# Gate steps moved to GpSimd, the first q and k loaded from two queues, and a per-step rank table in a fused attention and expert kernel

## The chip, the core and the metric

The kernel runs on one core of one Trainium2 chip. The metric is the time of one execution on the device in microseconds. Three timed runs of the kernel before gave 886.53, 890.16 and 890.55 us; their median, 890.16 us, is what the changed kernel is compared with. The engines are named as in the profile: PE is TensorE, DVE VectorE, ACT ScalarE, POOL GpSimd, SP SyncE (here a DMA queue).

## The reference

Attention over 8 batches of 8 heads, 576 positions and head size 64, in which scores further than `tau` below their row's maximum are dropped, and behind it a mixture of 8 experts on the 4608 rows of 512 that come out:

```python
scores = scale * np.matmul(q, k.transpose(0, 1, 3, 2))
thresh = np.max(scores, axis=-1, keepdims=True) - tau
scores = np.where(scores >= thresh, scores, -1000000000.0)
attn = np.exp(scores - np.max(scores, axis=-1, keepdims=True))
x = np.matmul(attn / (np.sum(attn, axis=-1, keepdims=True) + 1e-09), v)   # per head
...
do_compute = x @ w_skip > 0            # out = x elsewhere
logits = xc @ w_gate                   # xc = x[do_compute], 8 logits a token
e_idx = np.argmax(logits, axis=1)
for e in range(E):
    h = np.maximum(xc[mask] @ w1[e], 0.0)
    y[mask] = gate_w[mask, None] * (h @ w2[e])
out[do_compute] = xc + y
```

## The kernel before

**Attention.** Two heads make a pair (`g`, 32 in all, four to a batch). A pair has four chunks of 128 rows with two units each (one per head) and a ninth unit, the tail of 64 rows of both heads. A unit is a score block of 128 x 576 in one of three PSUM buffers `sps`: PE makes it (`score`, L601), DVE takes the maximum (`top`, L612), ACT the exponential (`expo`, L624), DVE multiplies it with the threshold mask (`mask`, L632), which frees the buffer. ACT rounds the chunk's `p` to f16 (`fph`, tile `hla`, L412), POOL makes the remainder (`fpl`, the split step, L683), SP transposes both by DMA (`turn`, L688, tile `PTa`), and PE multiplies with V (`av`, L751). The tail goes through PE instead (`tr` L705, `hi`, `lo` L713). V is brought to two f16 parts for each batch by `plan_v`: an absolute sum in two halves (`fsum`, ACT L494 or DVE L496), a scale (`fr`, ACT L555 or POOL L558), a cast, a remainder. `plan_out` copies the product out (`cpy`), makes the reciprocal (`fr`, L794) and on POOL the output rows `xb` (`fx`, L803) and tails `x` (`ft`, L816). `plan_logits` transposes these on PE (L859) and adds up the router's logits (L885).

**Gate.** For every two batches `plan_gate` turns nine logit columns a partition into expert, weight and slot of each token: a chain of small steps on tiles `ca` (128 x 72) and `gw` (128 x 9), all on DVE (L984 to L1080) but for the exponential (ACT) and a count over partitions (`rank`, PE), and at its end nine indirect DMAs from POOL (`sca`, L1108). The last two batches get two gates, one for batch 6, one for the rest. Behind batch 6's gate `plan_pick` chooses the fullest expert; `plan_early` loads its w1 in two halves (`lw`, and `second`, which is the load `raw` in L397), splits the weights in two parts (`hi` on ACT, `lo` on POOL, L1260), gathers 320 of its tokens (`ga`, L401) and runs its first layer (`L1`, PE L1311).

**Experts.** Behind the planned part, expert after expert in a fixed order; TensorE is busy nearly all of that time.

**What sets the order.** All of it up to the end of the first layer is recorded as steps with engines, durations and dependences. `Plan.run` (a list scheduler in Python, at build time) then goes through the steps: for each engine it looks at those that would be ready within `LOOK` = 0.1 us of the earliest, takes the one with the smallest key, and emits its instructions. So the keys order steps that compete for an engine, and each engine, SP's and POOL's queue too, works its instructions off in that order. A step that lists several engines goes to the one that can start it first. A key is a sum of named offsets from `ORDER`, with up to four values, chosen by the pair's place in its batch:

```python
pair = int(max(key.at, 0)) // STEP
return sum(c * ORDER[n][pair % len(ORDER[n])] for n, c in key.offs) if key.offs else key.at
```

`lock=True` marks DVE steps that the planner doesn't start while POOL is busy with a step of its own.

**Start.** SP issues the first pair's two loads (`load` in `plan_pair`, L437 and L438) as the first step of the plan. `warm` (L1407) keeps PE busy with 14 products of `ident` until the data is there.

Of the kernel before, what the change touches and what calls it, by code (L numbers as in the profile page):

```python
# [18 lines left out]
ALU = mybir.AluOpType  # L19
# [51 lines left out]
DLAT = 1.9  # L71
ORDER = dict(
    gk=(4349, 1.58e+04, 0, 0,),
    vm=(5384, 0, 0, 0,),
    tt2=(613.7, 1.58e+04, -3.449e+04, -1512,),
    hi2=(-4.346e+04, 3.034e+05, 3.133e+05, -5282,),
    lo2=(562.8, -2.259e+04, -9.309e+04, -4.515e+04,),
    eg=(-7406, -2.093e+05, 0, 0,),
    L1m=(2.989e+05,),
    ex=(-8.448e+04, 1.427e+04, -3.875e+04, -2e+04,),  # L80
    eav=(-1.313e+05, -1.651e+04, 4.278e+04, 1.964e+04,),
    ld=(-3.456e+04, 1.596e+05, -1.641e+05, 6.358e+04,),
    qs=(1.122e+05, 1717, -9.452e+04, 1.214e+04,),
    S=(-2.225e+05, -1.566e+05, -2.312e+04, -9.311e+04,),
    mx=(5534, 2.237e+05, -6.53e+04, -6820,),
    th=(-3.468e+04, 1.915e+05, -1.495e+05, 6.269e+04,),
    e=(-1.451e+05, -6.782e+04, -2141, -1.003e+04,),
    p=(-9031, -1.426e+04, -1.807e+05, -1.63e+05,),
    ph=(-1322, 1.222e+05, 4.057e+05, -9.705e+04,),
    pl=(-1.781e+05, 4.205e+04, 6250, -6.626e+04,),  # L90
    tt=(-2.69e+05, 6405, -2703, 9.818e+04,),
    av=(3.22e+05, 2.029e+04, 3.147e+04, 3.456e+04,),
    cp=(1.287e+04, -3.512e+04, -6.049e+04, -1.725e+05,),
    x=(-2.958e+04, -4.386e+04, 0.001192, 4.233e+04,),
    xw=(2433, 1831, 1.558e+04, -1.251e+05,),
    row=(-1594, 0, 0, 0,),
    rsp=(-1.029e+05, 0, 0, 0,),
    init=(-2.381e+05,),
    L1=(-1.868e+05,),
    sc=(-1.345e+05,),  # L100
    d0=(-1.107e+04,),
    v=(0.000848, 0, 0, -9374,),
    vsp=(-0.0004024, 0, 0, -1.917e+05,),
    V2=(0.002816, 0, 0, 0,),
    GS=(3.047e-10,),
)


class Key:


    def __init__(self, at=0.0, offs=()):
        self.at, self.offs = at, tuple(offs)

    def __add__(self, x):
        x = x if isinstance(x, Key) else Key(x)
        return Key(self.at + x.at, self.offs + x.offs)

    def __mul__(self, a):
        return Key(self.at * a, [(n, c * a) for n, c in self.offs])  # L120

    def __sub__(self, x):
        return self + x * -1

# [1774 lines left out]
```

## Time and profile before

| | |
|---|---|
| timed runs | 886.53, 890.16, 890.55 us (median 890.16) |
| the profiled execution | 882.97 us, its span 881.2 us |
| attention stage | from the first scores at 7.7 us to the last product with V at about 605 us |
| first layer of the early expert starts | 619.88 us |
| experts | to the end of the span |

The profile is of one execution. Its span is the time from the first to the last instruction; 1.8 us of the execution lie around it. "Busy" is the time in which an engine worked on an instruction; matmuls overlap, so PE's figure is an upper bound. A wait is idle time of an engine ahead of an instruction, with the instruction that ended it.

### The profile page before, as it was taken

To read this page: it belongs to the slowest core of one execution; us is meant where nothing else is said; L and a number is where in the kernel's file an instruction comes from. 1 tells how busy PE (TensorE), PEld (TensorE's weight loads), DVE (VectorE), ACT (ScalarE), POOL (GpSimd) and SP (SyncE) were. 2 spreads that over 40 slices of the span, in tenths; PEclk is the share of its full clock that TensorE was granted. 3 is DMA by queue.
4 is the path that set the end of the run, shared out by engine and by line. 5 is a ranking of instruction groups with operands and counts; after the bars stand their busy time and mean duration, and the time that the engine had idled before them with its cause. 6 is when DMAs were issued, how large, how long until landed. Compare 5 with 4: busy or idle time off the path is not lost. (4 is left out here: it accounts for less than half of the span.)

```text
span 881.2 us, 19509 instructions
## 1 busy us (share of the span) xinstructions
PE 790.0 (90%) x7294; PEld 668.1 (76%) x7294; DVE 680.2 (77%) x1284; ACT 602.9 (68%) x941; POOL 579.3 (66%) x384
## 2 busy tenths in 40 slices
PE   7789989888989997998988898774999999999997
PEld 5577868776867776786876777663879898999986
DVE  7988988898989799888989989881445463487772
ACT  5888978987988896897898788564334352454451
POOL 4767857857977784897685799468253464374453
PEclk9999999999999999999999999898899999999999
DMA  9899999999999999999999999588454544545440
GB/s 195 169 197 203 210 198 205 197 216 191 173 227 196 184 226 189 186 196 222 196 191 233 185 189 195 115 196 196 148 178 160 186 147 146 188 151 184 177 143 20
DMA packets 340031, 160.84 MB, mean 183 GB/s; under 512 B 311095, under 2 KB 311863, under 8 KB 339936
## 3 DMA queue, kind: packets, MB, share of 16 engines
q1 hardware_dynamic: 335312, 149.43, 82.4%
q0 software_dynamic: 4480, 10.15, 3.6%
q8 instruction: 59, 0.97, 0.5%
q14 instruction: 36, 0.29, 0.1%
q10 hardware_dynamic: 144, 0.00, 0.0%
HBM read 69.33 MB, written 15.21 MB: 96 GB/s over the span
## 5 line engine op out<-in xcount | busy, mean ns | idle before, releaser
L683 POOL TENSOR_TENSOR hla<-p,hla 128x1152 f16<-128x1152 f32 x128 | 303.9, 2377 | 122.6 <-ACT hla L412 103.0
L601 PE MATMUL sps<-KQ 128*128 128x288 f32 x1152 | 324.1, 423 | 50.7 <-DVE p L632 39.3
L601 PEld LDWEIGHTS sps<-KQ 128*128 128x128 f32 x1152 | 210.1, 194 | 115.7 <-issue 30.6
L612 DVE TENSOR_REDUCE mx<-sps 128x1 f32<-128x576 f32 x288 | 215.0, 750 | 45.1 <-PE sps L601 42.8
L624 ACT ACTIVATE ea<-sps,mx 128x576 f32<-128x576 f32 x288 | 206.5, 738 | 50.1 <-DVE mx L612 44.9
L632 DVE SCALAR_TENSOR_TENSOR p<-sps,tq,ea 128x576 f32<-128x576 f32 x256 | 200.2, 811 | 11.5 <-ACT ea L624 1.0
L412 ACT ACTIVATE hla<-p 128x1152 f16<-128x1152 f32 x128 | 148.5, 1161 | 34.0 <-DVE p L632 15.8
L751 PE MATMUL avp<-Vh,PTa 128*128 128x65 f16 (+1 forms) x2304 | 136.1, 198 | 10.4 <-DMA PTa<-hla 6.9
L751 PEld LDWEIGHTS <-PTa 128*128 128x128 f16 x3456 | 125.3, 99 | 25.7 <-DMA PTa<-hla 9.6
L751 PE MATMUL avp<-Vl,PTa 128*128 128x64 f16 (+1 forms) x1152 | 125.7, 197 | 0.5 <-DVE Vl L566 0.5
L1493 POOL TENSOR_TENSOR wl<-wr,wh 128x1024 fp32r<-128x1024 f32 x26 | 66.7, 2582 | 26.6 <-ACT wh L1492 18.7
L1573 POOL DMA_INDIRECT out<-o,ids x20 | 20.0, 998 | 80.9 <-DVE o L1572 26.8
L1533 PE MATMUL hps<-xh,wh 128*128 128x288 f32 (+4 forms) x224 | 69.1, 308 | 0.1
L1533 PE MATMUL hps<-xl,wh 128*128 128x288 f32 (+4 forms) x224 | 67.9, 303 | 0.0
L1533 PE MATMUL hps<-xh,wl 128*128 128x288 f32 (+4 forms) x224 | 67.8, 303 | 0.0
L1534 ACT ACTIVATE QK<-hps 128x288 fp32r<-128x288 f32 (+4 forms) x56 | 23.9, 427 | 60.8 <-PE hps L1533 60.2
L1492 ACT ACTIVATE wh<-wr 128x1024 fp32r<-128x1024 f32 x56 | 56.7, 1050 | 0.0
L1108 POOL DMA_INDIRECT lst<-rec,si x36 | 36.1, 1002 | 30.6 <-DVE pk L1365 13.1
L1493 DVE TENSOR_TENSOR wl<-wr,wh 128x1024 fp32r<-128x1024 f32 x30 | 50.2, 1688 | 6.9 <-ACT wh L1492 6.4
L1535 DVE SCALAR_TENSOR_TENSOR QK<-hps,QK 128x288 fp32r<-128x288 f32 (+4 forms) x56 | 26.1, 469 | 31.0 <-ACT QK L1534 30.8
L412 ACT ACTIVATE a<-avp 64x65 f32<-64x65 f32 (+1 forms) x128 | 36.9, 302 | 17.3 <-PE avp L751 16.0
L566 POOL TENSOR_TENSOR Vl<-vraw,Vh 128x1024 f16<-128x1024 f32 (+1 forms) x23 | 44.6, 1944 | 2.3 <-ACT Vh L412 2.3
(240 smaller groups left out, 1261.5 us busy)
## 6 DMA issues: line engine op xcount, KB each, us to landing
wr<-in_w SPq DMA_DIRECT2D x29, 1024.0 KB, 5.3
KQ<-in_kq SPq DMA_DIRECT2D x32, 320.0 KB, 4.8
KQ<-in_kq SPq DMA_DIRECT2D x32, 304.0 KB, 5.2
vraw<-in_vl SPq DMA_DIRECT2D x32, 256.0 KB, 5.2
out<-xb SPq DMA_DIRECT2D x32, 256.0 KB, 2.7
PTa<-hla SPq DMA_TRANSPOSE x256, 3.7
wn<-in_w SPq DMA_DIRECT2D x2, 1024.0 KB, 8.4
vraw<-in_vt SPq DMA_DIRECT2D x8, 128.0 KB, 4.8
```

The lines of the kernel that those rows point to most:

```text
L412: nc.scalar.activation(dst, src, AF.Copy)
L566: (nc.gpsimd if e == POOL else nc.vector).tensor_tensor(T["Vl", b][:, ts], vraw[:, ts], Vh[:, ts, 0:D], op=ALU.subtract)
L601: nc.tensor.matmul(ps[:, j, 0:HS], w, k[:, c0 : c0 + HS], start=True, stop=True, skip_group_check=True)
L612: nc.vector.tensor_reduce(T["mx", g][:, c, 0:1], bank(u), AX.XY, ALU.max, negate=True)
L624: nc.scalar.activation(e, bank(u), AF.Exp, bias=T["mx", g][:, c, 0:1])
L632: nc.vector.scalar_tensor_tensor(T["p", g, i][:, u].rearrange("p (a b) -> p a b", a=2), bank(u), T["tq", g][:, c : c + 1], T.pop(("e", g, ...
L683: nc.gpsimd.tensor_tensor(hl[:, lo0 : lo0 + w], T.pop(("p", g, i)).rearrange("p a b -> p (a b)"), hl[:, 0:w], op=ALU.subtract)
L751: nc.tensor.matmul(pv[:, o, 0:e], x[:, w_, :], y[:, vb, 0:e], start=not M and i % 2 + a + k == 0, stop=a == len(work) - 1 and k == 2, skip ...
L1108: sc = nc.gpsimd.indirect_dma_start(lst[:, :], bass.IndirectOffsetOnAxis(ap=G["si"][:, 0, t : t + 1], axis=0), G["rec"][:, t, :], None, bo ...
L1492: nc.scalar.activation(w[0][:, sl], rs, AF.Copy)
L1493: lo[q % 2].tensor_tensor(w[1][:, sl], rs, w[0][:, sl].bitcast(F32), op=ALU.subtract)
L1533: nc.tensor.matmul(hp_[:, 0:cap], w_, x, start=(i == 0), stop=(i == len(mm) - 1))
```

## The change

1. `ORDER` gets one entry for each step function, named by it, in place of shared offsets that were added up. A value is an integer, and an entry has one value or eight: four for the place in the batch, and four more for pairs from `LATE` = 24 on (the last two batches). The key is that value alone; equal keys go by the order of recording. All planned steps change rank by this.
2. The first pair's two loads are issued ahead of all else, one from SP, one from ACT's queue, ahead of the load of `tau`.
3. The gates of the first six batches (`side`, three gates) run their elementwise steps on POOL, grouped in three steps (`a1_, a2, a3b`; `a4, a5`; `c2, c3, c4`); reductions, the scan, exponent, counts and integer steps stay where they were. A comparison for equality becomes a subtraction and a comparison with zero. Two copies go: `a6` reduces to bf16 and `c5` reduces to integers directly. The gates of the last two batches stay on DVE, with the new steps.

```diff
+LATE = 24
 ORDER = dict(
-    gk=(4349, 1.58e+04, 0, 0,),
...
+    av_av=(157, 192, 172, 173, 193, 209, 37, 83),
+    chunk_expo=(129, 93, 108, 127, 55, 120, 77, 162),
...
-def place(key):
...
+def rank(at, fn):
+
+    path = [x.removeprefix("plan_") for x in fn.__qualname__.split(".") if x != "<locals>"][1:]
+    if path[-1] == "<lambda>":
+        path[-1:] = fn.__code__.co_freevars[:1]
+    r = ORDER["_".join(path)]
+    pair = int(max(at, 0)) // STEP
+    return r[(pair % HP + (HP if pair >= LATE else 0)) % len(r)]
...
+    def load_half(q, g, i):
+        r, c = halves[i]
+        q.dma_start(KQs[g % KQ][r, c], kq[g][r, 0 : c.stop - c.start])
+
+    load_half(nc.sync, 0, 0)
+    load_half(nc.scalar, 0, 1)
...
         def load():
-            nc.sync.dma_start(t[0:D, 0 : 2 * S + 2 * TL], kq[g][0:D])
-            nc.sync.dma_start(t[D:P, S:], kq[g][D:P, 0 : 2 * S + TL])
+            for i in range(2 if g else 0):
+                load_half(nc.sync, g, i)
...
+        side = pr < B // 2 - 1
+        ve = nc.gpsimd if side else nc.vector
...
-            nc.vector.tensor_tensor(G["eq"], G["lg"][:, :, 0:E], bc(G["mx"]), op=ALU.is_equal)
-            nc.vector.tensor_tensor(G["sh"], G["lg"][:, :, 0:E], bc(G["mx"]), op=ALU.subtract)
+            ve.tensor_tensor(G["sh"], G["lg"][:, :, 0:E], bc(G["mx"]), op=ALU.subtract)
+            ve.tensor_scalar(G["eq"], G["sh"], 0.0, None, op0=ALU.is_equal)
...
-            nc.vector.tensor_reduce(G["rs"], G["oh"], AX.X, ALU.add)
-            nc.vector.tensor_copy(G["rs16"], G["rs"])
+            with nc.allow_low_precision("small counts are exact"):
+                nc.vector.tensor_reduce(G["rs16"], G["oh"], AX.X, ALU.add)
...
-            nc.vector.tensor_tensor(G["si"][:, 0, 0:nt], G["slot"], G["ac2"], op=ALU.add)
+            with nc.allow_low_precision("whole numbers under 2 ** 24 are exact"):
+                nc.vector.tensor_reduce(G["si"][:, 0, 0:nt], G["rk"].rearrange("p e t -> p t e"), AX.X, ALU.add)
...
+        if side:
+            o = x = chain([o] + ring.take("ca", 1), (a1_, a2, a3b), 1, 1.2)
+            o = chain([o], (a3,), 2, 0.12, DVE)
+            o = chain([o], (a4, a5), 3, 0.6)
+            o = chain([o], (a6,), 4, 0.12, DVE)
...
+        if side:
+            o = chain([o, y], (c2, c3, c4), 9, 0.5)
```

What the ranks move is seen in three places. The first is SP's queue at the start (KQ is q and k of a pair, vraw a batch's V), before and with the change; with the change the first pair's other half is the first row of ACT's queue:

```order
L437 DMA KQ_105<-in_kq 64x1280
L438 DMA KQ_105<-in_kq 64x1216
L437 DMA KQ_106<-in_kq 64x1280
L438 DMA KQ_106<-in_kq 64x1216
L463 DMA vraw<-in_vl 128x512 x2
L467 DMA vraw<-in_vt 64x512
L470 DMA vraw<-in_vt 64x256
L420 DMA wgt<-in_wg 128x4x16
```

```order
L345 DMA KQ_96<-in_kq 64x1280
L345 DMA KQ_97<-in_kq 64x1280
L345 DMA KQ_97<-in_kq 64x1216
L517 DMA vraw<-in_vl 128x512 x2
L521 DMA vraw<-in_vt 64x512
L524 DMA vraw<-in_vt 64x256
L517 DMA vraw<-in_vl 128x512 x2
L474 DMA wgt<-in_wg 128x4x16
```

One issue of the first pair left SP, and all of the first V is now issued ahead of the router's weights.

The second is DVE in the first gate (mx is the maximum, p the mask, tq the threshold of a unit; ca and gw are the gate's tiles). Before:

```order
L993 TENSOR_TENSOR ca<-lg,gw 128x72
L994 TENSOR_TENSOR ca<-lg,gw 128x72
L612 TENSOR_REDUCE mx_120<-sps 128x1
L997 TENSOR_TENSOR ca<-ca,ioem 128x72
L998 TENSOR_SCALAR gw<-lg 128x9
L619 TENSOR_REDUCE tq_121<-mx_120 128x2
L1001 TENSOR_REDUCE gw<-ca 128x9
L1002 TENSOR_SCALAR gw<-gw 128x9
L632 SCALAR_TENSOR_TENSOR p<-sps,tq_121,ea 128x576 x2
L1005 TENSOR_TENSOR ca<-ioem,gw 128x72
```

With the change:

```order
L1036 TENSOR_REDUCE gw<-lg 128x9
L673 TENSOR_REDUCE tq_121<-mx_120 128x2
L686 SCALAR_TENSOR_TENSOR p<-sps,tq_121,ea 128x576 x2
L666 TENSOR_REDUCE mx_120<-sps 128x1 x2
L1053 TENSOR_REDUCE gw<-ca 128x9
L673 TENSOR_REDUCE tq_121<-mx_120 128x2
L666 TENSOR_REDUCE mx_120<-sps 128x1
L686 SCALAR_TENSOR_TENSOR p<-sps,tq_121,ea 128x576 x2
L1091 TENSOR_REDUCE gw<-ca 128x9
```

Six of the gate's small steps left this stretch of DVE's queue; its reductions stayed.

The third is POOL's queue at the end of attention (hla is a split step, xb and x the output rows and tails of a pair, wl the weights' second part, xg the gathered tokens). Before:

```order
L803 TENSOR_TENSOR xb<-a_114,z 128x4x128
L683 TENSOR_TENSOR hla<-p,hla 128x1152
L816 TENSOR_TENSOR x_6679<-a_114,z 64x128
L1108 DMA lst<-rec,si 36864x2
L1260 TENSOR_TENSOR wl_8352<-wr,wh_8246 128x512 x2
L1260 TENSOR_TENSOR wl_8356<-raw_8153,wh_8246 128x512
L1260 TENSOR_TENSOR wl_8352<-wr,wh_8246 128x512
L1260 TENSOR_TENSOR wl_8356<-raw_8153,wh_8246 128x512
L401 DMA xg_8413<-out,id_146 128x512 x2
L401 DMA xg_8413<-out,id_146 64x512
L803 TENSOR_TENSOR xb<-a_115,z 128x4x128
L1260 TENSOR_TENSOR wl_8352<-wr,wh_8246 128x512
```

With the change:

```order
L1184 DMA lst<-rec,si 36864x2
L737 TENSOR_TENSOR hla<-p,hla 128x1152
L1336 TENSOR_TENSOR wl_8160<-wr,wh_8153 128x512 x2
L737 TENSOR_TENSOR hla<-p,hla 128x1152 x2
L856 TENSOR_TENSOR xb<-a_114,z 128x4x128
L455 DMA xg_8303<-out,id_146 128x512 x2
L455 DMA xg_8303<-out,id_146 64x512
L869 TENSOR_TENSOR x_6666<-a_114,z 64x128
L1336 TENSOR_TENSOR wl_8160<-wr,wh_8153 128x512 x2
L856 TENSOR_TENSOR xb<-a_115,z 128x4x128
L869 TENSOR_TENSOR x_6666<-a_115,z 64x128
L1336 TENSOR_TENSOR wl_8443<-raw_8346,wh_8153 128x512 x2
```

The early gate's last record DMA (lst) now stands three split steps ahead of the end of attention instead of behind it, the gathers stand behind the last pair but one, and the last pair's xb and x stand ahead of four of the eight weight splits. On SP the second half of that w1 (raw) is now issued behind the last transposes, where before it was issued ahead of six of them.

## Rows read from the trace of the kernel before

**Rows 1.** Windows of the span: length, busy PE, PEld, DVE, ACT, POOL, clock, DMA.

```profile
100.00:200.00 100.00, 90.92 (x998) 74.37 (x995) 89.86 (x174) 85.74 (x133) 69.47 (x39) 1.00 1.10 206
600.00:620.00 20.00, 9.93 (x96) 7.61 (x96) 3.01 (x8) 4.79 (x12) 14.74 (x14) 0.70 0.77 224
750.00:800.00 50.00, 49.03 (x350) 47.09 (x349) 29.96 (x39) 22.68 (x39) 24.65 (x13) 1.00 0.54 186
```

**Rows 2.** Who waited for whom: us in total, times, longest.

```profile
POOL hla L683 <- ACT hla L412: 103.0, 63, 7.5
...
DVE mx L612 <- PE sps L601: 42.8, 75, 2.7
PE sps L601 <- DVE p L632: 39.3, 40, 2.8
```

**Rows 3.** Timeline of the start: start, us, engine, line, op.

```profile
0.74 0.59 SPq L437 DMA_DIRECT2D KQ<-in_kq  x1
...
1.39 0.57 SPq L438 DMA_DIRECT2D KQ<-in_kq  x1
...
1.78 6.06 PE L1407 MATMUL gps<-ident 128*128 128x128 f32 x28 [1.78 <-POOL ident masks.py:199]
...
7.09 0.55 DVE L445 TENSOR_SCALAR KQ<-KQ,tpos 128x640 f32<-128x640 f32 x1 [0.24 <-DMA KQ<-in_kq]
...
7.75 3.15 PE L601 MATMUL sps<-KQ 128*128 128x288 f32 x12
```

**Rows 4.** Groups by line on DVE, 40 to 555 us: busy us, mean ns.

```profile
L1076 DVE TENSOR_SCALAR si<-si 128x9 int32<-128x9 int32 x3 | 7.1, 2358 | 0.0
L1060 DVE TENSOR_TENSOR ca<-ca,co 128x72 f32<-128x72 f32 x3 | 6.1, 2045 | 0.0
...
L993 DVE TENSOR_TENSOR ca<-lg,gw 128x72 f32<-128x72 f32 x3 | 2.0, 683 | 0.1
...
L1065 DVE TENSOR_TENSOR ca<-ca 128x72 f32<-128x72 f32 x3 | 0.7, 222 | 0.0
...
L1002 DVE TENSOR_SCALAR gw<-gw 128x9 f32<-128x9 f32 x3 | 0.5, 154 | 0.0
```

**Rows 5.** The six windows of 17.5 us that hold the first three gates, summed.

```profile
sum 105.00, PE 87.50 PEld 71.97 DVE 98.47 ACT 81.23 POOL 63.10; mean PE 14.58 PEld 12.00 DVE 16.41 ACT 13.54 POOL 10.52
```

**Rows 6.** Groups by line and shape, 30 to 560 us (the last: DVE, from 40).

```profile
L683 POOL TENSOR_TENSOR hla<-p,hla 128x1152 f16<-128x1152 f32 x118 | 280.2, 2378 | 96.4 <-ACT hla L412 76.8 <-issue 7.7 <-DMA PTa<-hla 4.5
...
L816 POOL TENSOR_TENSOR x<-a,z 64x128 f32<-64x128 f32 x29 | 11.4, 393 | 1.6 <-POOL xb L803 0.7
L558 POOL TENSOR_TENSOR vraw<-vraw,vmx 128x1024 f32<-128x1024 f32 x4 | 7.6, 1896 | 2.7 <-ACT vmx L535 2.7
...
L494 ACT ACTIVATE Vl<-vraw 128x1280 f16<-128x1280 f32 x10 | 12.6, 1267 | 0.0
L555 ACT ACTIVATE vraw<-vraw,vmx 128x1024 f32<-128x1024 f32 x10 | 11.4, 1144 | 0.0
...
L496 DVE TENSOR_REDUCE vmx<-vraw 128x1 f32<-128x1280 f32 x4 | 5.9, 1478 | 0.0
```

**Rows 7.** A window in which a batch's V is split.

```profile
512.50:530.00 17.50, 15.71 (x183) 12.72 (x180) 15.08 (x30) 16.59 (x29) 17.31 (x11) 1.00 1.05 178
```

**Rows 8.** Timeline around the end of attention: SP, DVE, POOL, PE.

```profile
587.07 13.72 SPq L688 DMA_TRANSPOSE PTa<-hla  x6
...
605.39 1.25 POOL L1260 TENSOR_TENSOR wl<-raw,wh 128x512 fp32r<-128x512 f32 x1
...
606.31 0.22 DVE L794 RECIPROCAL z<-z 128x10 f32<-128x10 f32 x1 [0.79 <-ACT z L791]
...
606.80 1.04 POOL L401 DMA_INDIRECT xg<-out,id  x1 [0.16 <-issue]
...
610.43 1.06 POOL L803 TENSOR_TENSOR xb<-a,z 128x512 f32<-128x512 f32 x1
...
613.53 0.48 PE L859 MATMUL gps<-ident,x 128*128 128x128 f32 x1 [8.24 <-POOL x L816]
...
619.88 0.62 PE L1311 MATMUL sps<-xh,wh 128*128 128x320 f32 x1
```

**Rows 9.** DMA issues of the page: KB each, us from issue to landing.

```profile
wr<-in_w SPq DMA_DIRECT2D x29, 1024.0 KB, 5.3
```

More of the change, by code (lines that the diff above doesn't have):

```diff
@@ L94 @@
[L94 to L105, printed above, removed]
-)
[L109 to L123, printed above, removed]
-    def __rsub__(self, x):
-        return self * -1 + x
-    __radd__, __rmul__ = __add__, __mul__
@@ L131, in place @@
-def place(key):
-    if not isinstance(key, Key):
-        return key
-    pair = int(max(key.at, 0)) // STEP
-    return sum(c * ORDER[n][pair % len(ORDER[n])] for n, c in key.offs) if key.offs else key.at
-OFF = {n: Key(0, [(n, 1)]) for n in ORDER}
-GS = OFF["GS"]
+    ahead_op=(70,),
+    av_av=(157, 192, 172, 173, 193, 209, 37, 83),
+    blank_q=(217,),
+    chunk_expo=(129, 93, 108, 127, 55, 120, 77, 162),
+    chunk_mask=(70, 36, 66, 10, 102, 76, 46, 58),
+    chunk_score=(131, 114, 109, 142, 138, 115, 87, 16),
@@ L186, in op @@
         o.wait = len(o.deps)
+        o.no = len(self.ops)
         self.ops.append(o)
@@ L445, in scale @@
                 nc.vector.tensor_scalar(x, x, tpos, None, op0=ALU.mult)
-        o = pl.dma(k - OFF["ld"] if g else -100, load, ring.take("kq", KQ) + T["start"] + T["zero"][g % KQ : g % KQ + 1], [1.45, 1.45], 0.59)
-        T["in", g] = [pl.op(k - OFF["qs"], scale, [o], {ACT: 0.72} if g else {DVE: 0.45})]
+        o = pl.dma(k if g else -100, load, ring.take("kq", KQ) + T["start"] + T["zero"][g % KQ : g % KQ + 1], [1.45, 1.45], 0.59 if g else 0.3)
+        T["in", g] = [pl.op(k, scale, [o], {ACT: 0.72} if g else {DVE: 0.45})]
         if g == 0:
@@ L1082, in c7, with chain, run @@
             )
-        gs = GS if pr < B // 2 - 1 else 0.5
+        gs = 0 if side else 0.5
         o = pl.op(k, alloc, deps + T["settle"] + ring.take("gate", 2), {DVE: 0.14})
-        o = x = pl.op(k + gs, a1_, [o] + ring.take("ca", 1), {DVE: 0.31}, lock=True)
+        def chain(o, fs, n, d, e=POOL):
+            def run():
+                for f in fs:
+                    f()
+            run.__qualname__ = fs[0].__qualname__
+            return pl.op(k + gs * n, run, o, {e: d})
+        if side:
[3 more added lines that the diff above has]
+            o = chain([o], (a6,), 4, 0.12, DVE)
+        else:
+            o = x = pl.op(k + gs, a1_, [o] + ring.take("ca", 1), {DVE: 0.31}, lock=True)
+            for i, (f, d) in enumerate(((a2, 0.22), (a3, 0.12), (a3b, 0.1), (a4, 0.25), (a5, 0.15), (a6, 0.2))):
+                o = pl.op(k + gs * (2 + i), f, [o], {DVE: d}, lock=f not in (a3, a6))
         ex = pl.op(k + gs, exps, [x], {ACT: 0.16})
-        for i, (f, d) in enumerate(((a2, 0.22), (a3, 0.21), (a4, 0.18), (a5, 0.15), (a6, 0.33))):
-            o = pl.op(k + gs * (2 + i), f, [o], {DVE: d}, lock=f is not a3)
         rk = pl.op(k + gs * 7, rank, [o] + ring.take("gps", GPB), {PE: 0.06})
@@ L1098, in plan_gate @@
         ring.free("gps", [o])
+        if side:
+            o = chain([o, y], (c2, c3, c4), 9, 0.5)
         for i, f in enumerate((c2, c3, c4, c5, c6, c7)):
-            o = pl.op(k + gs * (9 + i), f, [o, y], {DVE: 0.13}, lock=f not in (c4, c6))
-            if f is c4:
+            if i < 3 and side:
+                continue
+            o = pl.op(k + gs * (9 + i), f, [o, y], {DVE: 0.13}, lock=f not in (c5, c6))
+            if f is c5:
                 ring.free("ca", [o, w])
```

220 lines of the change are left out of this document (147 added, 73 removed).

## The prediction

> **What bounds the kernel now.** I read the windows first, since the busy shares of the whole page mix two kernels in one. In attention PE is busy 90.92 of 100 us, DVE 89.86 and ACT 85.74 [rows 1]: no engine is full, three are nearly so. With the experts PE is busy 49.03 of 50 us, and nothing off PE matters there. Between the two lies a hole: from 600 to 620 us PE is busy for 9.93 of 20 us, at a mean granted clock of 0.70, between its two levels of 1.2 and 2.4 GHz [rows 1]. The table of waits says what the missing tenth of attention is: PE waits 39.3 us in all for masks that free a score buffer, and DVE waits 42.8 us for scores [rows 2]. It is a round trip between two engines over three buffers, so time that is taken off DVE comes back only in part, and an order that suits the round trip better or worse can move the time as well. POOL is not in it: it stands idle for 103.0 us ahead of its split steps because ACT has not rounded the chunk yet [rows 2]. Then I looked at the four places that the change touches: the start, the gates, V, and the end of attention.
>
> **The start.** The first pair's loads are issued at 0.74 and 1.39 us [rows 3]; from two queues the second goes out some 0.65 us sooner. Its data is waited for at 7.09 us, by the scale on DVE, for 0.24 us only. The first scores start at 7.75 us, but PE is held by its warm-up products until 1.78 + 6.06 = 7.84 us [rows 3], which the change leaves as they are. The cover for a late load is this warm-up: if it were gone, 0.24 to 0.65 us would be won. On SP the first V's loads pass the router's weights and two writes, for which nothing waits until the first pair's output is there. So **0 us** (bounds 0 and -0.65).
>
> **The gates.** Eleven DVE instructions leave each of three gates: L1060, and ten that run from L993 with 2.0 us in three calls down to L1002 with 0.5 us [rows 4]. Together they are 14.2 us of DVE (6.1 for L1060, and 2.0, 1.3, 0.8, 0.7, 0.7, 0.6 and four of 0.5, the rows between these being sorted by cost). L1060 shows what such steps really cost: 2045 ns, against 222 ns for L1065, of the same shape [rows 4]. Some of that is waiting for a POOL split step of 2378 ns [rows 6]. The Trainium skill states a rule for it (SBUF — State Buffer, "Who interferes with whom"): a DVE instruction with two SBUF inputs, or in a two-port mode, and a GpSimd instruction that reads SBUF exclude each other for the whole instruction, and the one issued second waits. The trace agrees: L1076, which stays on DVE, takes 2358 ns, nearly the length of a split [rows 4, 6].
>
> What is the time worth? In the six windows with gates DVE is busy 98.47 of 105 us and PE only 87.50, 83.3% [rows 5], against 90.9% in the stage at large [rows 1]: PE loses 0.076 x 105 = 8 us to the three gates. That is the upper bound of the gain. The lower is nothing, if DVE then waits for scores instead. The steps that leave are about half of the gates' DVE time (L1076 alone keeps 7.1 us), and L1060's block is in the middle of the chain of masks, so I take a little more than half: **-5 us**.
>
> POOL takes 11 instructions a gate, 33 in all. The trace has no POOL step of 72 elements: by proportion to a split (2378 ns for 1152) one would take 0.15 us, and the smallest broadcast product there is takes 0.39 us [rows 6], so 5 to 13 us; I take 0.27 us each, 9 us, between the two because a fixed part is to be expected and most are smaller than the product of 128. The Trainium skill speaks against this move (GPSIMD Engine Reference, "4.1 Engine selection"): elementwise work with two inputs is about twice as slow on GpSimd. Twice the unblocked DVE time of these steps (14.2 less three blocks of about 1.8, 8.8 us) would be an estimate of 18 us by that page instead of 9; the sum stays the same as long as POOL has room. It has: 63.10 of 105 us busy in these windows [rows 5]. So 0 us; without that cover it would be the whole 9. The steps wait on DVE reductions in between, and behind each waiting step stands a split on POOL; nobody but the transposes and the products with V, one to two chunks later, waits for it.
>
> **V.** Where a step may go to several engines, the new ranks place it otherwise. Counting instructions in the two programs, five scales of 1024 and three absolute sums leave ACT (5 x 1144 + 3 x 1267 = 9.5 us), six scales go to POOL (6 x 1896 = 11.4 us), three sums to DVE (3 x 1478 = 4.4 us) [rows 6]; one scale and one cast of the first batch leave DVE, which I bound by ACT's 1.1 us each. DVE is one of the two engines of the round trip, so net 4.4 - 2 = 2.4 us there count by half: **+1 us**. Bounds: -9.5 if ACT decides, +11.4 if POOL does.
>
> **The order in the middle.** All 32 pairs get another interleaving. The work between the engines is the same and the pattern reads much alike: two maxima, threshold, two masks, with a third maximum drawn ahead here and there. I find no row that says which of the two suits the chip better, so **0 us**, with a quarter of PE's 39.3 us of waiting [rows 2] either way: 10 us as bounds.
>
> **The end of attention.** Here the order matters plainly. The last pair's reciprocal is done at 606.31 + 0.22 = 606.53 us, but its `xb` starts on POOL at 610.43, because three gathers (from 606.80 on) stand ahead of it; PE's transposes of the tail come at 613.53 after 8.24 us of idleness, and the early expert's first layer at 619.88 [rows 8]. With the change the gathers lie behind the last pair but one, while the attention still runs, and `xb` and `x` go ahead of four weight splits. Then `xb` and `x` end about 1.06 + 0.39 us after 606.5, at 608.0 [rows 6, 8]. Two chains remain. Four splits of 1.25 us [rows 8] behind that end at 613.0. And the second half of w1, now issued behind the last transposes (587.07 + 13.72 = 600.8 us), lands 5.3 us later [rows 9], at 606.1, which is in time for them. PE's two rounds of transposes and logits, 6.35 us from 613.53 to 619.88 in the old order, start at 608.0 and end by 614.4 at the latest. So the first layer starts at about 613 to 614.4 instead of 619.9: **-6 us** (bounds -7, and 0 if the last chunk itself comes later). What is late next is the split of w1, then the weights' landing. All that follows is PE work and moves along.
>
> **The sum.** 0 - 5 + 1 + 0 - 6 = -10 us. The profiled execution took 882.97 us, so 873 by its measure; the median of the timed runs lies 7 us above it, 890.16 us, and against that the forecast is **880 us**. I call no change what lies within 0.5% (4.5 us), about what a measurement of this kernel can tell: 885.7 to 894.6 us.
>
> **The rivals.**
> *The round trip gains too.* If the new interleaving takes a quarter off PE's waits (10 us), the time is 870 us, and with the gates' full 8 us 867. For it: separate ranks for the late pairs, where PE's share is lowest. Against it: the patterns of DVE's queue are nearly the same.
> *DVE's freed time turns into waiting.* DVE already waits 42.8 us for scores [rows 2]; if the gates give nothing, V costs DVE its full 4.4 us, and only the end is won: 890.2 + 4.4 - 6 = 888.6 us, no change.
> *Blocks move to other steps.* The scan and the count offsets of a gate stay on DVE with inputs in SBUF, and POOL is fuller. By the rows a block costs some 2.2 us (2358 less 160) [rows 4]; two more in each of three gates make 13 us: 880 + 13 = 893 us. Against it: the trace of before shows such a small step unblocked too, L1065 with 222 ns [rows 4]. By the Trainium skill's rule on the shared pair, cited above, the steps with two inputs in SBUF are the ones that can be caught.
> *POOL becomes the bound (slower).* While a batch's V is split, POOL is busy for 17.31 of 17.5 us already [rows 7], and six of seven later batches get 1.9 us more of it there. From the point at which a split step ends later than the buffers of rounded chunks allow, ACT's rounding, the mask and the scores stop behind it. Then the 11.4 us of V and the 9 us of gate steps all show, and the gates win nothing: 890.2 + 20.4 - 6 = 904.6 us; with half of it, 894.4. Against it: in that same window PE is busy for 15.71 of 17.5 us, 89.8%, hardly less than elsewhere.
>
> **How the numbers follow.** The forecast's case (gates and end are won, 873 to 887 us) has 0.50; the round trip's gain 0.16; freed time turning into waiting 0.12; moved blocks 0.06; POOL as bound 0.16, of which some three quarters end above 894.6. Faster by over 0.5%: 0.16 and 0.46 of the forecast's 0.50, 0.62. Slower by over 0.5%: 0.12 of POOL's case and 0.04 of the others, 0.16. The rest, 0.22, is no change. The range goes from 862 us, the forecast with the gates' full 8 us, V's gain of a few us by ACT and the round trip's 10, to 897 us, POOL's case at a little over half of its price; about 1 in 10 lies on either side.
>
> **What would show it.** Right: the first scores again at about 7.7 us; L1060's successor gone from DVE, and PE's share in the stretches with gates near 87% or more; POOL steps of the gate at 0.15 to 0.4 us each; the first layer's first matmul 8 to 10 us behind the last product with V (now 15); the experts' stage as long as before. Wrong: PE's waits for masks or DVE's waits for scores grown by more than 5 us between 40 and 555 us; idle time ahead of ACT's rounding that POOL ends; gate steps on POOL of 0.6 us or more; or a first layer that still starts 15 us after the last product with V, held by the second half of w1.

## The result, and the profile after

The change makes the kernel slower: 894.45 us (median of 19 runs, 889.2 to 899.42) against 886.0 us for the kernel before on the same occasions (19 runs, 878.81 to 896.32). The ratio is **1.0114, 95% interval [1.0085, 1.0142]**. Runs of one kernel differ by up to 2%, so versions are compared by their ratio to the kernel before, measured beside them. The 890.16 us that the forecast started from are the median of the first three of the 19; 10 us less than 886.0 would be 876. The profiled execution of the changed kernel took 889.2 us, the shortest of its 19, its span 887.3 us (before 881.2).

First the sums that the prediction named as signs. The table of waits of the changed kernel (us in total, times, longest):

```profile
POOL hla L737 <- ACT hla L466: 81.7, 45, 8.1
...
DVE mx L666 <- PE sps L655: 44.1, 67, 4.8
...
PE sps L655 <- DVE p L686: 33.1, 45, 3.6
...
PE avp L805 <- DMA PTa<-hla: 12.6, 13, 1.9
...
PE sps L655 <- ACT ea L678: 5.5, 2, 3.8
```

Against [rows 2], POOL idles less (103.0 before), PE waits less for masks (39.3), DVE hardly more for scores (42.8). By these sums the change looks like a gain. Two waits of PE that the prediction did not name grew: for exponentials (no such row before), and for transposed chunks. Before:

```profile
PE avp L751 <- DMA PTa<-hla: 6.9, 12, 1.3
```

What also grew is in the page's first part and its clock: the same 7294 matmuls keep PE busy for longer, at a mean granted clock of 0.973 (before 0.979). The first row of the page, before and changed:

```profile
PE 790.0 (90%) x7294; PEld 668.1 (76%) x7294; DVE 680.2 (77%) x1284; ACT 602.9 (68%) x941; POOL 579.3 (66%) x384
```

```profile
PE 797.5 (90%) x7294; PEld 675.3 (76%) x7294; DVE 671.8 (76%) x1251; ACT 596.1 (67%) x931; POOL 599.3 (68%) x423
```

So the place has to be found by time, not by sums. The last step of each pair's tail on DVE (it writes `TM`, L713 before, L767 after) marks the pace. Time between the starts of these steps in the profiled executions, in us, with three of the versions below:

| stretch | before | changed | a_unblock | u_best | u_gdve |
|---|---|---|---|---|---|
| start to pair 8 | 171.26 | 172.77 | 174.26 | 173.61 | 173.71 |
| 8 to 12 (first gate) | 74.69 | 78.42 | 74.44 | 72.37 | 73.23 |
| 12 to 16 | 71.54 | 73.61 | 73.12 | 70.92 | 72.76 |
| 16 to 20 (second gate) | 74.71 | 73.25 | 74.04 | 74.76 | 72.04 |
| 20 to 24 | 70.18 | 70.62 | 72.03 | 70.43 | 71.04 |
| 24 to 28 (third gate) | 72.96 | 71.42 | 73.35 | 73.67 | 77.13 |
| 28 to 31 (batch 6's gate) | 61.74 | 65.35 | 59.83 | 55.49 | 56.67 |
| pair 31's tail to first layer | 22.80 | 21.09 | 20.64 | 21.14 | 19.20 |
| first layer to end of span | 261.32 | 260.77 | 260.49 | 260.51 | 261.42 |

The changed kernel loses 3.7 us at the first gate and 3.6 us at the gate of batch 6, wins 1.5 us at each of the other two, and wins 1.7 us at the end of attention; the stretches between are 0.4 to 2.1 us longer.

Each column is one execution, and the early gates differ as much between executions of one order. a_end below runs the changed kernel's program up to the end of attention: its second gate took 78.20 us in place of 73.25. In b_c2, b_c6 and b_best below, which keep the old order, the first gate took 77.9 to 79.1 us in place of 74.69. Only the loss at batch 6's gate is there in each of them: 65.35 and 64.47 us in the changed order, 60.9 to 61.7 in the old one.

The two losses look alike. The timeline of the changed kernel at the first gate (start, us, engine, line, op; in brackets the idle time before and what ended it):

```profile
200.48 2.37 POOL L737 TENSOR_TENSOR hla<-p,hla 128x1152 f16<-128x1152 f32 x1
200.54 2.33 DVE L1097 TENSOR_SCALAR gw<-gw 128x9 f32<-128x9 f32 x1
...
203.08 1.39 DVE L666 TENSOR_REDUCE mx<-sps 128x1 f32<-128x576 f32 x2
203.90 1.41 ACT L678 ACTIVATE ea<-sps,mx 128x576 f32<-128x576 f32 x2 [2.27 <-DVE mx L666]
...
205.60 0.82 PE L655 MATMUL sps<-KQ 128*128 128x288 f32 x1 [3.85 <-ACT ea L678]
```

POOL finishes its gate steps and starts a split at 200.48; DVE comes to a step on nine elements 0.06 us later and is held until the split ends. Behind it stand two maxima, the exponentials and the masks, and PE stands still for 3.85 us. Batch 6's gate, which stayed on DVE:

```profile
554.50 4.70 POOL L737 TENSOR_TENSOR hla<-p,hla 128x1152 f16<-128x1152 f32 x2 [1.79 <-DVE mx L666]
...
555.06 0.16 DVE L673 TENSOR_REDUCE tq<-mx 128x2 f32<-128x4 f32 x1
555.15 1.78 DVE L1045 TENSOR_TENSOR ca<-lg,gw 128x32 f32<-128x32 f32 x1
...
556.96 2.27 DVE L1046 TENSOR_SCALAR ca<-ca 128x32 f32<-128x32 f32 x1
559.15 1.53 DVE L686 SCALAR_TENSOR_TENSOR p<-sps,tq,ea 128x576 f32<-128x576 f32 x2
```

Two gate steps meet two splits in a row, one each; the masks that would have freed two score buffers start 4 us late. The clock falls as well. Two rows of PE's timeline, twelve score matmuls with a short idle time before them and twelve behind this gap, and the window of 5 us that holds most of the second (busy PE, PEld, DVE, ACT, POOL, granted clock, DMA):

```profile
539.59 3.15 PE L655 MATMUL sps<-KQ 128*128 128x288 f32 x12 [1.54 <-DVE p L686]
...
560.10 5.91 PE L655 MATMUL sps<-KQ 128*128 128x288 f32 x12 [3.57 <-DVE p L686]
```

```profile
560.00:565.00 5.00, 4.90 (x10) 3.54 (x11) 3.15 (x8) 2.53 (x5) 3.21 (x2) 0.50 0.53 65
```

PE stood still for 3.57 us and then worked at 0.50, the lower level: 2.76 us more for the same twelve. With the gap that is 6.3 us behind the two caught steps. The old order has a caught step at this gate too, but one alone (L1002, 2.33 us at 558.69), with a gap of 2.77 us behind it (562.52).

The end of attention, on POOL, PE and DVE:

```profile
613.56 0.22 PE L805 MATMUL avp<-Vh,TM 128*128 128x130 f16 x1
...
615.65 2.50 POOL L1336 TENSOR_TENSOR wl<-wr,wh 128x512 fp32r<-128x512 f32 x2
...
618.10 1.05 POOL L856 TENSOR_TENSOR xb<-a,z 128x512 f32<-128x512 f32 x1
619.23 0.39 POOL L869 TENSOR_TENSOR x<-a,z 64x128 f32<-64x128 f32 x1
...
619.68 0.48 PE L912 MATMUL gps<-ident,x 128*128 128x128 f32 x1 [1.89 <-POOL x L869]
```

The first layer starts at 626.53, 12.75 us behind the last product with V (613.78); before it was 14.93 us (604.95 to 619.88, [rows 8]). Two weight splits still stand ahead of the last pair's `xb`. The last product with V before:

```profile
604.73 0.22 PE L751 MATMUL avp<-Vh,TM 128*128 128x130 f16 x1
```

The start:

```profile
0.73 0.57 ACTq L345 DMA_DIRECT2D KQ<-in_kq  x1
...
1.34 0.60 ACTq L350 DMA_DIRECT2D taub<-in_tau  x1
...
6.34 0.15 DVE L352 TENSOR_SCALAR tpos<-taub 128x1 f32<-128x1 f32 x1 [2.83 <-DMA taub<-in_tau]
...
7.54 0.54 DVE L499 TENSOR_SCALAR KQ<-KQ,tpos 128x640 f32<-128x640 f32 x1
...
8.18 0.72 PE L655 MATMUL sps<-KQ 128*128 128x288 f32 x2 [1.07 <-issue]
```

`tau`, which the scale needs, now lands behind the first pair's half on ACT's queue, DVE waits 2.83 us for it with a row of small steps behind, and the first scores start at 8.18 us in place of 7.75 [rows 3].

### The profile page after: what moved, and what is told of

Its sections match the earlier page's. It is cut to its first block, busy times and chain, and to the rows that moved or that the text cites. A ratio compares the mean times of both kernels' runs of the same rounds, so it can differ in the third digit from the quotient of the medians.

```text
span 887.3 us, 19506 instructions
## 1 busy us (share of the span) xinstructions
PE 797.5 (90%) x7294; PEld 675.3 (76%) x7294; DVE 671.8 (76%) x1251; ACT 596.1 (67%) x931; POOL 599.3 (68%) x423
## 5 line engine op out<-in xcount | busy, mean ns | idle before, releaser
L737 POOL TENSOR_TENSOR hla<-p,hla 128x1152 f16<-128x1152 f32 x128 | 304.0, 2378 | 101.1 <-ACT hla L466 81.7
L805 PEld LDWEIGHTS <-PTa 128*128 128x128 f16 x3456 | 128.3, 100 | 32.5 <-DMA PTa<-hla 14.7
L805 PE MATMUL avp<-Vh,PTa 128*128 128x65 f16 (+1 forms) x2304 | 138.9, 199 | 15.0 <-DMA PTa<-hla 12.6
L805 PE MATMUL avp<-Vl,PTa 128*128 128x64 f16 (+1 forms) x1152 | 128.6, 198 | 2.2 <-DVE Vl L620 2.2
L856 POOL TENSOR_TENSOR xb<-a,z 128x512 f32<-128x512 f32 x32 | 33.3, 1045 | 19.0 <-DVE z L847 11.2
```

Of the source, the lines that this page charges most:

```text
L737: nc.gpsimd.tensor_tensor(hl[:, lo0 : lo0 + w], T.pop(("p", g, i)).rearrange("p a b -> p (a b)"), hl[:, 0:w], op=ALU.subtract)
L805: nc.tensor.matmul(pv[:, o, 0:e], x[:, w_, :], y[:, vb, 0:e], start=not M and i % 2 + a + k == 0, stop=a == len(work) - 1 and k == 2, skip ...
L856: nc.gpsimd.tensor_tensor(T["x", b].rearrange("p c (h d) -> p c h d", d=D)[:, :, 2 * hp : 2 * hp + 2], T["a", g][:, 0:NM, :, 0:D], T["z", ...
```

## The experiments

**The theory:** the loss is made of small DVE steps that the new order puts right behind the start of a split, with masks behind them. **Rivals:** the gate steps on GpSimd cost by themselves; the row of record DMAs on POOL makes splits late; the loss is spread over the new order. All edits marked "own order" leave the planner's steps, ranks and durations alone and only change on which engine, or how much later, a step issues its instructions, so that all else keeps its place.

### Two blocked places taken away, and rivals beside it

**a_unblock** (the changed kernel, own order):

```diff
 def a1_():
-    ve.tensor_tensor(G["sh"], ...)
-    ve.tensor_scalar(G["eq"], G["sh"], ...)
+    pe = nc.vector if t0 else nc.gpsimd
+    pe.tensor_tensor(G["sh"], ...)
+    pe.tensor_scalar(G["eq"], G["sh"], ...)
 def b2():
-    nc.vector.tensor_scalar(G["se"], ...)
+    ve.tensor_scalar(G["se"], ...)
```

> The changed kernel in its own order, with two small steps taken off DVE's queue at the places where they were blocked: the sum's offset in the early gates (2.33 us at 200.54) and the first two steps of batch 6's gate (1.78 and 2.27 us at 555.15) are issued on GpSimd. If such blocks are the loss, TensorE's two longest gaps (3.85 us before 205.60, 3.57 us before 560.10) and the half clock behind them (some 1.6 and 2.8 us) go: 5 to 11 us faster than the changed kernel, ratio to before 1.000 to 1.006. If the loss is spread over the new interleaving, within 2 us of it: 1.009 to 1.014.

Measured: 0.9994 [0.9962, 1.0027]. Against the changed kernel's 1.0114 that is some 10 us less, as much as the whole loss. In the profile the gap ahead of the first gate's scores is 1.61 us in place of 3.85, that at batch 6's gate 1.61 in place of 3.57, and the two stretches of the table fall to 74.44 and 59.83 us, 9.5 us together (the spans of the two profiles differ by 5.1 us, the medians, 894.45 and 884.24 us, by 10.2):

```profile
204.84 2.18 PE L655 MATMUL sps<-KQ 128*128 128x288 f32 x8 [1.61 <-ACT ea L678]
...
559.30 3.15 PE L655 MATMUL sps<-KQ 128*128 128x288 f32 x12 [1.61 <-DVE p L686]
```

So of the 6.3 us at batch 6's gate, 2.0 us of gap and the 2.76 us of slower matmuls went with the block. The theory holds. PE's waits for transposed chunks are still 14.1 us here, and the record DMAs still stand in their row, so what was won back lay in neither.

**a_gates_dve** (own order):

```diff
-        ve = nc.gpsimd if side else nc.vector
+        ve = nc.vector
```

> The changed kernel in its own order, with the elementwise steps of the three early gates issued on DVE again, at the places that the order gives them. Changed against before is 1.0114 (889.2 us profiled). If the move to GpSimd gains what the prediction said (5 us) and the loss lies elsewhere, this run is slower than the changed kernel by 5 us or more, since the steps are also open to blocks of up to 2.4 us each: ratio to before 1.017 or more. If the move itself costs (steps on GpSimd, hand-overs between the engines), it is faster by 2 us or more: 1.009 or less.

Measured: 1.0105 [1.0058, 1.0151], neither: the same as the changed kernel. The move as a whole is worth nothing in this order. In the trace other steps are caught than before: the first gate's step is not (pairs 8 to 12 take 74.48 us), but DVE's steps in the third gate are, and pairs 24 to 28 take 77.30 us.

**a_spread** (own order; `fpl` is the split step):

```diff
+            def put(sca=sca):
+                if side:
+                    pend.append(sca)
+                else:
+                    sca()
...
 def fpl():
     nc.gpsimd.tensor_tensor(...)
+    if pend:
+        pend.pop(0)()
```

> The changed kernel in its own order, but each record DMA of the three early gates is issued behind a later split step, one per split, in place of up to four in a row ahead of a split (223.24 to 228.06 us). If the row of DMAs makes the splits and then TensorE late, the pairs behind the gates (11, 19 and 26, which take 5.5, 4.3 and 4.3 us more than before) get back 1 to 3 us each: 3 to 8 us faster than the changed kernel, ratio to before 1.002 to 1.008. If GpSimd has room there, no change: 1.010 to 1.013.

Measured: 1.0122 [1.0061, 1.0184]: no gain. By itself this run settles little, because the blocks moved with the DMAs: in its profile the first gate's step is free, the second gate's is caught (2.26 us at 351.84, a gap of 3.77 us behind it), at batch 6's gate other steps are caught (1.28 us at 565.79, 2.32 us at 572.37), and PE has new gaps of 2.50 and 3.03 us (244.14, 397.58). That the row of record DMAs is not the loss rests on a_unblock, which leaves it as it is.

**b_gates** (the kernel before with its own keys and the change's `plan_gate`, planned anew):

> The kernel before with its own keys and start, and only the gate part of the change (the three early gates' steps on GpSimd, planned anew with the old keys). By the prediction's term 5 us faster than before: ratio 0.994 (0.991 to 1.000). If the gate steps on GpSimd cost rather than gain, 1.002 or more. If the interleaving that a new plan happens to give decides, anything between 0.985 and 1.015, and the trace shows blocks at other places than before.

Measured: 1.0169 [1.0117, 1.0221], slower than before by 15 us. This alone could mean that gate steps on GpSimd cost much, or that a new plan does.

### What a new order costs by itself

**b_look** (the kernel before, planned anew):

```diff
-LOOK = 0.1
+LOOK = 0.12
```

> The kernel before with nothing changed but the planner's window LOOK, 0.12 us in place of 0.10: the same steps and keys, another interleaving. The prediction put the middle's new order at 0 with 10 us either way. If an order that was not chosen for this chip costs by itself, this run is slower than before by 5 us or more (1.006 and up), with blocked small steps at new places, much as the run b_gates. If the interleaving hardly matters, 0.997 to 1.003, and the 13 us of b_gates are the cost of gate steps on GpSimd.

Measured: **1.0264 [1.0218, 1.0311]**, 23 us slower, with the same steps and keys; a few steps that may go to several engines went to another (DVE has 1282 instructions for 1284, ACT 943 for 941). A new plan alone can cost more than b_gates lost, so b_gates says nothing about GpSimd. And here too PE's waits for masks would have misled (table of waits of b_look, and the first row of its page):

```profile
DVE mx L612 <- PE sps L601: 49.8, 76, 3.3
...
PE sps L601 <- DVE p L632: 31.3, 47, 2.0
...
PE avp L751 <- DMA PTa<-hla: 15.9, 15, 2.7
```

```profile
PE 801.0 (89%) x7294; PEld 678.8 (75%) x7294; DVE 671.5 (74%) x1282; ACT 605.0 (67%) x943; POOL 581.7 (65%) x385
```

PE waits less for masks than before (39.3), but DVE waits 7.0 us longer for scores and PE 9.0 us longer for transposed chunks, and PE is busy 11 us longer with the same matmuls, at a mean granted clock of 0.969 (before 0.979). The part of the expectation on blocked steps did not come true: in the three early gates one step alone is caught (2.38 us at 199.91). So this loss is not made of such blocks, and what makes it stays open.

**a_late** (`LATE = 32`: no ranks of their own for the last two batches, planned anew):

> The changed kernel with LATE = 32: all pairs use the first four values of each rank, the last two batches have none of their own. The changed kernel took 65.35 us from pair 28 to 31 (before 61.74). If the late pairs' own ranks cause that, this run is 3 us or more faster than the changed kernel, ratio 1.008 or less. If they help at the end of attention, as the prediction had it, it is slower: the last output rows and the gathers come later, 1.015 or more. If it only moves which gate steps stand behind a split step, anything between.

Measured: 1.0174 [1.0122, 1.0225], slower still. The time as a whole does not decide on the late ranks, because the new plan also changed the pairs ahead of them: in this profile all three early gates have a gap of 3.77 to 3.87 us ahead of the same scores. Pairs 28 to 31 took 57.75 us in place of 65.35, though a step of batch 6's gate is caught there too (2.20 us at 572.73). So the late ranks may be what makes that gate dear; it was not tried with all else kept.

### The end of attention and the start

**a_end** (own order but for POOL's queue; `held` keeps the first two weight splits back until the tail of pair 30 is due, and that tail until pair 31's rows):

```diff
 def lo(...):
-    nc.gpsimd.tensor_tensor(w_l(d, fs), ...)
+    held.append(emit) if n < 2 else emit()
...
+def ft():
+    if g == NG - 2:
+        for f in held:
+            f()
+        held[:] = [ft_]
+    else:
+        ft_()
+def fx():
+    if g == NG - 1:
+        held.pop()()
+    fx_()
```

> The changed kernel in its own order but for GpSimd's queue at the end of attention: all four splits of the first half of w1 behind the gathers, and the last pair but one's tail behind them, so that the last pair's output rows and tail stand behind no weight split. In the changed kernel two splits ran at 595.36, ahead of the last two chunks' splits, and two at 615.65, between the tail of the last pair but one and the last pair's rows (618.10), and TensorE waited until 619.68 for the tail. If these places are what holds the end, the last split step ends 0.6 to 1 us sooner and the transposes of the tail start 2.5 us sooner: 2.5 to 3.5 us faster than the changed kernel, ratio to before 1.007 to 1.009, and the first layer about 10 us behind the last product with V (13.0 in the changed kernel). If something else ends last there (landing of the gathers, the second half of w1), 1.010 to 1.013.

Measured: 1.0073 [1.0039, 1.0108], in the expected range, though its interval overlaps that of the changed kernel. The profile is clearer. POOL has pair 31's tail ready 4.69 us behind the last product with V (620.71 after 616.02) in place of 5.84 (619.62 after 613.78), and the first layer starts 11.93 us behind it in place of 12.75: 1.2 us won at the tail, 0.8 at the first layer, not 2.5. (The 13.0 us of the expectation count from the start of that product.) The two rounds of transposes and logits, some 7 us at the lower clock (granted 0.50 from 620.4 to 628.0), stay.

The same profile shows by how little a block comes or stays away. Up to this point it is the changed kernel's program, step for step. The second gate in the changed kernel:

```profile
352.69 0.30 DVE L1076 TENSOR_TENSOR_SCAN ca<-seg,ca 128x72 f32<-128x72 f32 x1
...
352.79 2.37 POOL L737 TENSOR_TENSOR hla<-p,hla 128x1152 f16<-128x1152 f32 x1 [0.43 <-ACT hla L466]
...
355.43 0.72 PE L655 MATMUL sps<-KQ 128*128 128x288 f32 x2 [1.68 <-ACT ea L678]
```

and in a_end:

```profile
351.49 2.37 POOL L737 TENSOR_TENSOR hla<-p,hla 128x1152 f16<-128x1152 f32 x1 [0.27 <-ACT hla L466]
...
351.54 2.48 DVE L1092 TENSOR_TENSOR_SCAN ca<-seg,ca 128x72 f32<-128x72 f32 x1
...
356.46 0.48 PE L655 MATMUL sps<-KQ 128*128 128x288 f32 x1 [3.86 <-ACT ea L678]
```

The scan that starts 0.10 us ahead of the split takes 0.30 us, the one that starts 0.05 us behind it 2.48 us. So the 1.5 us that the changed kernel won at its second gate belong to that execution.

**u_end** (a_unblock and a_end together, and the load of `tau` ahead of `load_half(nc.scalar, 0, 1)`):

> The kernel of a_unblock with the end of a_end, and with the load of tau again ahead of the first pair's half on ScalarE's queue. If blocks, end and start add up: a_unblock's 0.9994 less 2.5 to 3.5 us and 0.4 us, ratio 0.995 to 0.996, first scores at 7.7 us in place of 8.15. If the end is held by something else, 0.998 to 1.000.

Measured: 0.9975 [0.9935, 1.0016]: between the two expectations. The first scores start at 7.77 us, as before, and the first layer 11.69 us behind the last product with V, about what a_end showed.

### Blocks in the old order

**b_c2** (the kernel before, own order):

```diff
 def c2():
-    nc.vector.tensor_tensor(G["rk"], ...)
+    (nc.gpsimd if pr < B // 2 - 1 else nc.vector).tensor_tensor(G["rk"], ...)
```

> The kernel before in its own order, with one step of the early gates (L1060, 2045 ns on VectorE, blocked) issued on GpSimd at the same place, between two split steps. The prediction took the gates' gain from this block ('in the middle of the chain of masks', 5 us for the three gates): ratio to before 0.994. The trace of before speaks against it: behind the block at 339.45 TensorE is busy for 5.00 of 5 us (340 to 345) at full clock, so VectorE's lost 1.8 us are covered: 0.998 to 1.002.

Measured: 0.9993 [0.9951, 1.0036]. The step on which the prediction rested its gate term (L1060, [rows 4]) is blocked for 2 us in three gates, and taking it off DVE wins nothing that can be measured. The second gate shows it with nothing else changed: 74.79 us in place of 74.71. In the first gate another step is caught in this profile, the count offsets `co` (2.21 us at 193.16), and that gate takes 77.91 us.

**b_c6** (the kernel before, own order; the step keeps its place but for one pair of masks):

```diff
+def c6():
+    pend.append(c6_) if pr < B // 2 - 1 else c6_()
...
 def mask(u):
     nc.vector.scalar_tensor_tensor(...)
+    if u == units[-1] and pend:
+        pend.pop()()
```

> The kernel before in its own order, but the integer step that is blocked for 2.36 us in each early gate (L1076) is issued behind the next chunk's two masks in place of ahead of them. Behind it TensorE waits 2.46 us in each of three gates (205.33, 351.70, 496.59), and in two of them the clock of the next 5 us is 0.66 to 0.72. If a block costs where masks that free a score buffer are next behind it, 2 to 3 us are won at each gate: 6 to 9 us, ratio 0.990 to 0.993. If the round trip gives the freed time back, 0.997 to 1.002.

Measured: 0.9977 [0.994, 1.0014], 2 us, which lies in the range of the second expectation. On the spot it does what it should. Windows at the three gates, before:

```profile
205.00:210.00 5.00, 4.67 (x38) 3.53 (x39) 3.40 (x9) 2.94 (x4) 2.63 (x3) 0.66 1.01 225
350.00:355.00 5.00, 3.30 (x8) 2.30 (x9) 3.88 (x9) 2.61 (x4) 2.00 (x3) 0.72 1.06 238
495.00:500.00 5.00, 3.41 (x52) 2.92 (x53) 4.81 (x11) 2.72 (x4) 2.20 (x3) 1.00 1.01 215
```

and in b_c6:

```profile
205.00:210.00 5.00, 5.00 (x67) 4.10 (x66) 4.39 (x11) 3.04 (x4) 2.21 (x1) 0.94 0.81 152
350.00:355.00 5.00, 4.75 (x33) 3.75 (x31) 4.80 (x13) 3.71 (x7) 2.82 (x2) 1.00 1.35 155
495.00:500.00 5.00, 4.75 (x31) 3.67 (x31) 4.80 (x15) 3.88 (x7) 2.65 (x2) 1.00 1.07 201
```

The gaps of 2.46 us are gone, and the low clock that stood behind two of the three. Over the whole gate less is left: the second gate's stretch is 73.16 us, 1.6 less than before, the third's 73.43, 0.5 more. The first gate's is 78.39 us, 3.7 more: ahead of the moved step the count offsets `co` are caught here, which were free in the profile of before (0.16 us at 191.93):

```profile
194.84 2.25 DVE L1056 TENSOR_TENSOR co<-cnt,eoff 128x8 f32<-128x8 f32 x1
```

**b_best** (b_c2 and b_c6, and the second first load from ACT's queue behind `tau`):

> The kernel before in its own order with the steps of b_c2 and b_c6 both, and the first pair's second load from ScalarE's queue behind that of tau. If the gates' cost in the old order is the one block ahead of the masks, as b_c6: 0.990 to 0.993. If both blocks count, 0.985 to 0.988. If a step that moves only makes another one blocked, 0.997 or more.

Measured: 0.9952 [0.9911, 0.9993], between the expectations: with both steps moved, and the load, the old order is faster by half a per cent. Which of the three does it can't be told, as the intervals of b_c2, b_c6 and b_best overlap; in this profile too `co` is caught in the first gate (2.22 us).

### The version that beats both

**u_best** (u_end, with the edit of b_c6 for the first four gates, and the same for `p3`, the comparison that picks the early expert, L1242):

> The kernel of u_end (0.9975) with two more steps issued behind the next masks in place of ahead of them: the integer step of the first four gates and the comparison that picks the early expert. In u_end both are blocked at the end of attention (1.5 to 1.8 us) and TensorE waits 1.37 and 1.30 us behind them. If such blocks are what is left of the change's loss, 2 to 5 us faster than u_end: 0.992 to 0.995. If not, 0.996 to 1.000.

Measured: **0.9897 [0.986, 0.9933]**, 876.04 us (median of 12): 1% faster than before, 2% faster than the change as it came, and better than expected. Pairs 28 to 31 take 55.49 us (changed 65.35).

**u_gdve** (u_best with the early gates on DVE again):

> The kernel of u_best (0.9897) with the elementwise steps of the three early gates on VectorE again, at the same places. If the move to GpSimd is worth the prediction's 5 us once the longest blocks are gone, this run is 5 us or more slower than u_best: ratio to before 0.995 or more. If the move is worth nothing and only the place of each step against the split steps counts, 0.988 to 0.992.

Measured: 0.9937 [0.9905, 0.9968], between the two, and the intervals of the two versions overlap. The largest difference in the profile is in the third gate (77.13 against 73.67 us), where two of the steps that came back are caught:

```profile
483.58 2.34 DVE L1070 TENSOR_SCALAR gw<-lg 128x9 f32<-128x9 f32 x1
...
494.93 2.28 DVE L1140 TENSOR_TENSOR ca<-ca 128x72 f32<-128x72 f32 x1
```

In the second gate the version with the steps on DVE is the faster one (72.04 against 74.76 us); the other stretches differ by up to 1.9 us, either way. So the move seems to gain where a step would have been blocked; that it gains there only is not shown by one execution of each.

## Why the prediction was wrong

The forecast was 880 us, 10 us faster; the median is 894.45 us, near the upper end of the range (897), and the kernel 1.1% slower than before, 8.5 us between the medians. By its steps:

**The gates, -5 us: the step that failed.** "L1060's block is in the middle of the chain of masks, so I take a little more than half." b_c2 shows that this block is covered. The one that cost PE something, L1076, stayed on DVE in the change. The three early gates gave +3.7, -1.5 and -1.5 us in the profiles, +0.7 in sum (other executions give other sums, as said above), and in a_gates_dve the move as a whole is worth nothing. What decides is whether DVE comes to such a step while a split runs, how much of the split is left, and what stands behind the step: a block ahead of maxima and masks leaves PE a gap of 2.5 to 3.9 us and, in several cases, some microseconds at the lower clock; one behind which PE still has work costs nothing (b_c2). The prediction priced blocks by their length, and PE's share in gate windows as if DVE's load made it.

**The rival that came true had 0.06.** "Blocks move to other steps" gave 893 us. Its mechanism was right; the run a_unblock shows that taking away two places of this kind wins as much as was lost. That its time is so near is luck: it counted six blocks of 2.2 us in the three early gates, and nothing for the gap and the clock. The dearest block is in batch 6's gate, which the change leaves on DVE, with new steps in it. The rows of caught steps above show that the caught step ends with the split; among them are steps with a single tensor input (L1097, 2.33 us; L1046, 2.27 us), where the prediction took "the steps with two inputs in SBUF" for those that can be caught. A reduction goes through: the one at 555.06 takes 0.16 us inside a split. The page of the Trainium skill that the prediction named (SBUF — State Buffer, "Who interferes with whom") lists this too: `tensor_scalar` can enter a two-port mode and so contend with GpSimd, `tensor_reduce` never does on this chip; the trace agrees with both.

**The order in the middle, 0 with bounds of 10 us: the bound was too small.** b_look moves the time by 23 us with hardly a change in the work. The bound was a quarter of PE's waits for masks, and that sum fell in both slower versions. In b_look 11.0 of the 20.2 us of longer span are PE's busy time, at the lower mean clock, and 9.2 are idle time; which places cause it is not shown.

**The end of attention, -6 us: right in kind, a third of the size.** The first layer follows the last product 2.2 us sooner (12.75 for 14.93). Two weight splits that the prediction left out stood ahead of `xb` (2.5 us), and the two rounds of transposes and logits took 6.85 us. The last product itself came 8.8 us later.

**The start, 0: nearly.** 0.43 us later, because `tau` went behind the half; the term's bounds left a loss out. By the end of pair 1's tail the difference is 0.13 us.

**POOL's cost, 0, 9 us covered: right.** The gate's 33 steps take what was expected, 202 to 409 ns each where 270 were taken, 10.2 us in all (dearest and cheapest group by line and shape below). POOL has room: it still waits 81.7 us for ACT's rounding, and ACT's rounding waits 4.4 us for POOL (before 2.7).

```profile
L1046 POOL TENSOR_SCALAR ca<-ca 128x72 f32<-128x72 f32 x3 | 1.2, 409 | 0.3
...
L1056 POOL TENSOR_SCALAR gw<-gw 128x9 f32<-128x9 f32 x3 | 0.6, 202 | 0.2
```

So the rival of POOL as the bound, 0.16, did not happen; that it gave 894.4 us with half of its price is luck. The experts' stage is as long as before, as forecast (260.77 for 261.32 us). **V's +1 us** was not tried by itself and stays open; the stretches in which POOL took over more of V's scales (12 to 16, 20 to 24) are 2.1 and 0.4 us longer, which the order alone could do.

The tests that the text set for itself were half blind: "PE's waits for masks or DVE's waits for scores grown by more than 5 us" did not come true in a kernel that lost 1.1%. A sign of being right did: "PE's share in the stretches with gates near 87% or more". In the windows of [rows 5], in which the changed kernel is some 2 to 7 us behind in its work, PE was busy for 94.08 of 105 us, 89.6%, and matmuls that run at the lower clock count as busy:

```profile
sum 105.00, PE 94.08 PEld 77.74 DVE 93.76 ACT 81.21 POOL 75.33; mean PE 15.68 PEld 12.96 DVE 15.63 ACT 13.54 POOL 12.56
```

## What to carry to other kernels

Price a blocked small step by what stands behind it on its queue and by the gap and clock of TensorE there, not by its own length: a block of 2 us cost nothing where PE still had work (b_c2), those at two other places some 10 us together. When a planner's input changes, take the new interleaving as a cost of its own (here up to 2.6%); to learn what an edit is worth, keep the order and move single steps. And a step that is moved behind the next masks rather than to another engine can be all that is needed.

## What the runs showed of the hardware

- Whether a small DVE step is held for a whole split of 2.37 us is decided by some 0.15 us: 0.30 us when it began 0.10 us ahead of the split, 2.48 us when 0.05 us behind it, in two programs that are alike up to there. The step `co` of the first gate is free in the profile of before (0.16 us) and held for 2.2 us in those of b_c2, b_c6 and b_best.
- A step is held to the end of the split, however short it is: 2.33 us for nine elements a partition that came 0.06 us behind the start, 1.78 us for one that came 0.65 us behind it. A reduction beside a split took its 0.16 us.
- Behind 3.57 us in which it stood still, TensorE ran twelve score matmuls in 5.91 us at a granted clock of 0.50, where 3.15 us are usual; behind a gap of 1.54 us it did not slow down (the row at 539.59). Behind gaps of 2.46 us in three gates of the kernel before, the granted clock of the next window was 0.66, 0.72 and 1.00.
